# Retention attention and an ELU feed-forward on one Trainium2 core: order of state matmuls and bank copies, the pipeline of the first batch, and how block-diagonal states are written

## The chip, the cores and the metric

The kernel runs on one core of a Trainium2 chip. The metric is device time in microseconds for one execution; lower is better. The engines in the profile are PE (TensorE, matmuls; PEld is its weight load), DVE (VectorE), ACT (ScalarE), POOL (GpSimd) and SP (SyncE, which here only issues DMAs).

## The reference

```python
def _attn_ref(q, k, v):                     # 8 batches, 8 heads, 576 positions, 64 wide
    scores = scale * np.matmul(q, k.transpose(0, 1, 3, 2))
    gamma = 1.0 - 2.0 ** (-5.0 - np.arange(H, dtype=np.float32))
    Dmat = np.where(rel >= 0, gamma[:, None, None] ** rel[None, :, :], 0.0)
    ret = scores * Dmat[None, :, :, :]
    return np.matmul(ret, v).astype(np.float32)

def _moe_ref(x, w_in, w_out):               # 4608 tokens, 512 -> 2048 -> 512
    h = x @ w_in
    g = np.where(h > 0.0, h, alpha * (np.exp(np.minimum(h, 0.0)) - 1.0))
    return (g @ w_out).astype(np.float32)
```

The heads of the attention output are put side by side, so that x is 4608 x 512. The attention has no softmax: scores are multiplied by a decay that depends on the distance alone and vanishes above the diagonal.

## The kernel before

**Attention in units.** Because the decay gamma^(i-j) splits into gamma^i times gamma^-j, queries and keys are scaled once and the causal product becomes linear. A batch is cut into five units: four of 256 positions by four heads (`T` is 0 or 1 for the half of the sequence, `w` is 0 or 1 for the half of the heads) and a tail of 64 positions with all eight heads. Forty units in all; units 0 to 3 are the first batch without its tail, unit 4 (`FT`) is that tail, units 5 to 8 the second batch. Within a unit of 256 positions there are two chunks of 128 (`c` is 0 or 1). Each position's output is the masked product within its chunk (`scores`, `masks`, `values`) plus the queries times the sum of k·v over all earlier chunks (`inter`). `state` computes k·v of the unit's two chunks, `prefix` adds them to the running total: `mid` is the sum up to the middle of the unit, `end` up to its end, both on DVE. They are then written in bf16 as block-diagonal matrices of two heads (`s_mid`, `s_end`), whose other blocks were set to zero once at the beginning, so that `inter` handles two heads in one matmul.

**What a unit goes through.** `load` issues three DMAs for q, k and v on SP. `cast` scales q and k by the decay tables into bf16 (`qkn`, two instructions each, one for every `e`) and converts v (`vn`); without `split` all on POOL, with it q on DVE and v on the engine that `split` names, issued later by `later[u]`. `turn_pe` transposes q and k by TensorE through a bank of `ps_h` and copies them out (`qkT`; q on DVE, k on ACT); from unit 9 on `turn` does it by a transposing DMA instead.

**Banks.** `x0` and `x1` hold the unit's output (columns 0 to 255) and the states (columns 256 to 383) in the same bank, one buffer each (`ps_x`); `sc` has one buffer, `ps_h` three, `ps_m` one. Dependences are kept by bank: a TensorE write into a bank waits for the reads of it that came before. `put_x` (line 319) copies both output banks to `xt`, the transposed x of the feed-forward, normally on ACT.

**Order.** All matmuls are pinned in program order through `mm`. `soft` pins the other engines' instructions too as long as `early[0]` is true, that is up to `finish(FT + 2)` at line 537; from then on a planner places the instructions of DVE, ACT and POOL by its own estimate of when they are ready. Each engine runs its queue strictly in that order. All DMAs on SP are pinned.

**The stages.** (1) Lines 472 to 499: the first batch, one unit a round; `warm` issues matmuls on zeros between them. `last_of_start` finishes unit 3 in two halves of heads. (2) Lines 500 to 519: 16 pieces of w_in and 16 of w_out come through eight staging buffers (`wst`) and are converted on POOL, while `ffn1` and `ffn2` of the first 512 tokens run. (3) Lines 520 to 537: the rest of that group's `ffn2`, with units 4, 5 and 6 between. (4) From line 538: `ffn1` of the second group in two parts, then groups of 512 tokens, in which `step` (line 561) puts a unit's `stretch` between the slots of feed-forward matmuls. In `stretch(u)` the matmuls of unit u and of unit u-1's output are issued together: inter(u-1), scores(u), values(u-1), then the copies `put_x(u-1)`, then state(u) and prefix(u).

Of the kernel before, what the change touches and what calls it, by code (L numbers as in the profile page):

```python
# [17 lines left out]
def kernel(  # L18
# [15 lines left out]
    P = 128  # L34
# [33 lines left out]
    def soft(ins):  # L68
        return pin(ins) if early[0] else ins
# [57 lines left out]
                            channel_multiplier=-1)  # L127


    s_mid, s_end = [], []  # L130
    for i in range(2):
        for lst, n in ((s_mid, 1), (s_end, 2)):
            row = []
            for j in range(n):
                s = const.tile([P, 2, P], BF16, name=f"sbd{i}{j}{n}")
                nc.gpsimd.memset(s, 0.0)
                row.append(s)
            lst.append(row)

    w_in_sb = const.tile([P, KJ, DF], BF16, name="w_in_sb")  # L140
    w_out_sb = const.tile([P, NFT, DM], BF16, name="w_out_sb")
# [13 lines left out]
        soft(engines[eng](w_out_sb[:, f, :], t))  # L155


    rawt, natt, trt, ptt, score_ps, later, total = {}, {}, {}, {}, {}, {}, {}
# [6 lines left out]
    def load(u):  # L165
        if u >= NS:
            return
        b, T, w, tail = unit(u)
        if tail:
            rqk = raw.tile([P, H, D], FP32, name="rqt", tag="rqt", bufs=2)  # L170
            rv = raw.tile([ST, H, D], FP32, name="rvt", tag="rvt", bufs=2)
            for dst, src in ((rqk[:ST], q), (rqk[ST:], k), (rv, v)):
                pin(nc.sync.dma_start(dst, src[b, :, FT * P :, :].rearrange("h p d -> p h d")))
        else:
            rqk = raw.tile([P, 2, 4, 2, D], FP32, name="rqk", tag="rqk")
            rv = raw.tile([P, 4, 2, D], FP32, name="rv", tag="rv")
            for dst, src in ((rqk[:, 0], q), (rqk[:, 1], k), (rv, v)):
# [6 lines left out]
    def cast(u, split=None):  # L184
        if u >= NS:
            return
        b, T, w, tail = unit(u)
        rqk, rv = rawt.pop(u)
        if tail:
            qkn = nat.tile([P, H, D], BF16, name="qkt", tag="qkt", bufs=2)  # L190
            vn = nat.tile([ST, H, D], BF16, name="vt", tag="vt", bufs=2)
            g = gq[:, FT].unsqueeze(2).to_broadcast([P, H, D])
            for hs in (slice(0, H // 2), slice(H // 2, H)):
                soft(nc.gpsimd.tensor_tensor(qkn[:, hs], rqk[:, hs], g[:, hs], ALU.mult))
            soft(nc.gpsimd.tensor_copy(vn, rv))
        else:
            qkn = nat.tile([P, 2, 2, 4, D], BF16, name="qkn", tag="qkn")
            vn = nat.tile([P, 4, 2, D], BF16, name="vn", tag="vn", bufs=5)
            for i, tab in enumerate((gq, gk)):
                eng = nc.vector if split and i == 0 else nc.gpsimd  # L200
                x = rqk[:, i].rearrange("p h e d -> p e h d")
                g = tab[:, 2 * T : 2 * T + 2, 4 * w : 4 * w + 4].unsqueeze(3).to_broadcast([P, 2, 4, D])
                for e in range(2):
                    soft(eng.tensor_tensor(qkn[:, i, e], x[:, e], g[:, e], ALU.mult))  # L204
            later[u] = lambda: soft(engines[split or "p"](vn, rv))  # L205
            if not split:
                later.pop(u)()
        natt[u] = qkn, vn

    def turn_tile(u):  # L210
        n = 4 if unit(u)[3] else 8
        trt[u] = tpool.tile([P, n, P], BF16, name="qkT", tag=f"qkT{n}")
        return n
# [6 lines left out]
            turn_tile(u)  # L220
            pin(nc.sync.dma_start_transpose(trt[u], flat(u)))

    def turn_pe(u, parts=(0, 1)):
        n = turn_tile(u) if 0 in parts else 8
        for i in parts:
            if i * 4 < n:
                p = ps_h.tile([P, 4, P], BF16, name="ptr", tag="ph")
                for j in range(4):
                    lo = (i * 4 + j) * P
                    pin(nc.tensor.transpose(p[:, j], flat(u)[:, lo : lo + P], ident))  # L230
                soft(engines["vs"[i]](trt[u][:, i * 4 : i * 4 + 4], p))  # L231

    def queries(u, rows, hl, c):

# [52 lines left out]
    def inter(u, hls=(0, 1), to=None):  # L287
        b, T, w, tail = unit(u)
        if tail:
            for hp in range(HP):  # L290
                o = xps[0][:, hp * ST : (hp + 1) * ST]
                acc_x(0, 2, o, s_end[hp // 2][1][:, hp % 2], trt[u][:, hp, :ST])
            return
        for c in range(2):
            if T + c == 0:
                continue
            s = s_mid[w][0] if c else s_end[w][0]
# [39 lines left out]
    def drop(u):  # L337
        natt.pop(u)
        ptt.pop(u)
        trt.pop(u)  # L340
# [9 lines left out]
                        o = 2 * P + hl * D  # L350
                        acc_x(c, i, xps[c][i * D : (i + 1) * D, o : o + D], qkn[cs, 1, e, 2 * hl + i], vn[cs, 2 * hl + i, e])

    def prefix(u):
        b, T, w, tail = unit(u)
        st = [x[:, 2 * P : 3 * P].rearrange("p (h d) -> p h d", h=2) for x in xps]
        mid = rpool.tile([P, 2, D], FP32, name="mid", tag="mid")
        end = rpool.tile([P, 2, D], FP32, name="end", tag="end")
        if T == 0:
            soft(nc.vector.tensor_copy(mid, st[0]))
        else:  # L360
            soft(nc.vector.tensor_tensor(mid, st[0], total[w], ALU.add))  # L361
        soft(nc.vector.tensor_tensor(end, st[1], mid, ALU.add))
        total[w] = end
        for dst, src in ((s_mid[w][0], mid), (s_end[w][T], end)):
            for i in range(2):
                r = slice(i * D, (i + 1) * D)
                soft(nc.gpsimd.tensor_copy(dst[r, :, r], src[r]))  # L367

    def last_of_start(u):

        sc = score_ps.pop(u)
        pt = ppool.tile([P, 2, 2, 2 * P], BF16, name="pt", tag="pt")
        ptt[u] = pt
        second = [ps_h.tile([P, 512], FP32, name="o2", tag="ph") for _ in range(2)]
        for hl in range(2):
            soft(nc.vector.tensor_tensor(
                pt[:, :, hl], sc.rearrange("p i (h n) -> p i h n", h=2)[:, :, hl],
                mask.rearrange("p k e r -> p (k e r)").unsqueeze(1).to_broadcast([P, 2, 2 * P]), ALU.mult,
            ))
# [90 lines left out]


    for u in range(FT):
        load(u)
    cast(0, split="s")
    turn_pe(0)
    scores(0)
    later.pop(0)()
    new_x()
    state(0)
    prefix(0)  # L480
    for u in range(1, FT):
        cast(u, split="p" if u == FT - 1 else "s")
        masks(u - 1)
        warm(2)
        turn_pe(u, (0,))
        new_x()
        inter(u - 1)
        values(u - 1)
        put_x(u - 1)
        drop(u - 1)  # L490
        turn_pe(u, (1,))
        later.pop(u)()
        warm(1)
        scores(u)
        state(u)
        prefix(u)
    warm(2)
    new_x()
    last_of_start(FT - 1)
    for i in range(6):  # L500
        w_in_piece(i, "p")
# [123 lines left out]
```

## Time and profile before

| | us |
|---|---|
| median of three runs (370.94 to 371.69) | 371.31 |
| profiled execution, whole | 371.33 |
| its span on the core | 369.6 |

The profile counts from the start of the span. Its page gives busy times by engine, the waits tell what released an engine that stood, and a timeline row has the start, the time, the engine, the line of the source, what is written from what, the number of instructions, and in brackets how long the engine had been idle and what ended it. A row with several instructions is their merged time. Line 72 is the helper through which every matmul goes, so matmuls are told apart by the names of their tiles: `x<-vn,qkn` is state, `x<-pt,vn` values, `x<-qkT,sbd` inter, `sc<-qkT` scores, `ph` ffn1, `pm` ffn2.

### The profile page before, as it was taken

What the parts mean: (1) busy time and instruction counts of PE and PEld (TensorE: products, weight loads), DVE (VectorE), ACT (ScalarE), POOL (GpSimd) and SP (SyncE); (2) the same over time, 40 slices, a digit from 0 to 9 for tenths busy, and PEclk for the clock granted to TensorE, in tenths of its full rate; (3) what the DMA queues carried; (4) which work ended last, traced back from release to release, by engine and by line L of the source; (5) the groups of instructions that cost most, each with busy time, mean ns of one, the idle gap of its engine ahead of it and who ended that gap; (6) DMA issues with size and microseconds to landing.
All of it is one profiled execution on the core that took longest, in us unless ns stands there. A gap on an engine that the chain in (4) does not pass through costs nothing.

```text
span 369.6 us, 7943 instructions
## 1 busy us (share of the span) xinstructions
PE 318.6 (86%) x3044; PEld 161.4 (44%) x3087; DVE 203.2 (55%) x380; ACT 176.1 (48%) x360; POOL 180.7 (49%) x385
## 2 busy tenths in 40 slices
PE   3779996287877899999999999999999999999995
PEld 1443443144555444444444444444444444444442
DVE  3546725167574777556556666655655565454500
ACT  3226632156443655655555555555555555655511
POOL 6558955984699687056553665366511110010000
PEclk9978999679899999999999999999999999999999
DMA  7908999984799987906559656932220000010012
GB/s 222 330 22 253 394 267 299 268 185 113 185 202 222 276 136 209 231 29 101 145 148 185 155 170 145 235 89 77 67 65 28 30 31 29 28 58 29 28 61 83
DMA packets 100294, 53.87 MB, mean 146 GB/s; under 512 B 44448, under 2 KB 93600, under 8 KB 100256
## 3 DMA queue, kind: packets, MB, share of 16 engines
q1 hardware_dynamic: 97696, 44.97, 50.4%
q0 software_dynamic: 2560, 8.39, 6.1%
q8 instruction: 24, 0.39, 0.5%
q14 instruction: 14, 0.11, 0.1%
HBM read 36.70 MB, written 9.44 MB: 125 GB/s over the span
## 4 chain that ended last, share of the span: by engine, by line
PE 69%; POOL 11%; ACT 9%; DVE 5%; issue 4%; DMA 2%; DVEq 0%; POOLq 0%; ACTq 0%
PE ph L72 30%; PE pm L72 30%; PE x L72 6%; POOL qkn L204 4%; ACT xt L334 4%; PE sc L72 3%; DMA wst<-in_moe_w_in_dram 2%; ACT ot L453 1%; POOL w_in_sb L150 1%; ACT ph L434 1%; DVE pt L281 1%; POOL vn L205 1%; ACT qkT L231 1%; DVE g L443 1%; DVE em L436 1%
## 5 line engine op out<-in xcount | busy, mean ns | idle before, releaser
L72 PE MATMUL ph<-xt,w_in_sb 128*128 128x512 bf16 (+2 forms) x612 | 149.4, 365 | 3.7 <-DVE g L443 0.9
L72 PE MATMUL pm<-w_out_sb,g 128*128 128x512 bf16 x564 | 142.7, 379 | 2.9 <-ACT ot L453 1.5
L432 ACT ACTIVATE e<-ph 128x512 f32<-128x512 f32 (+2 forms) x152 | 87.3, 574 | 116.8 <-PE ph L72 103.1
L72 PEld LDWEIGHTS <-w_in_sb 128*128 128x128 bf16 x640 | 60.1, 99 | 66.1 <-issue 4.5
L72 PEld LDWEIGHTS <-g 128*128 128x128 bf16 x576 | 55.7, 98 | 70.4 <-issue 7.1
L441 DVE SCALAR_TENSOR_TENSOR g<-e,ph 128x512 bf16<-128x512 f32 (+2 forms) x80 | 50.3, 633 | 59.3 <-ACT ph L434 58.6
L456 POOL DMA_DIRECT2D out_dram<-ot x32 | 18.1, 566 | 98.1 <-ACT ot L453 71.6
L436 DVE TENSOR_SCALAR em<-e 128x512 bf16<-128x512 f32 (+2 forms) x76 | 36.0, 474 | 51.4 <-ACT e L432 51.4
L443 DVE SCALAR_TENSOR_TENSOR g<-ph,em 128x512 bf16<-128x512 f32 (+2 forms) x80 | 50.6, 637 | 3.2
L434 ACT ACTIVATE ph<-ph 128x512 f32<-128x512 f32 (+2 forms) x76 | 43.3, 570 | 0.0
L334 ACT CAST xt<-x 128x256 bf16<-128x256 f32 (+1 forms) x72 | 24.1, 414 | 38.2 <-PE x L72 38.1
L204 POOL TENSOR_TENSOR qkn<-rqk,gk 128x256 bf16<-128x256 f32 x64 | 40.2, 635 | 3.5
L281 DVE TENSOR_TENSOR pt<-sc,mask 128x1024 bf16<-128x1024 f32 x31 | 37.8, 1218 | 7.0 <-PE sc L72 7.0
L204 POOL TENSOR_TENSOR qkn<-rqk,gq 128x256 bf16<-128x256 f32 x52 | 31.1, 618 | 13.4 <-PE x L72 13.3
L453 ACT COPY ot<-pm 128x512 f32<-128x512 f32 x36 | 21.1, 589 | 21.8 <-PE pm L72 21.8
L205 POOL CAST vn<-rv 128x512 bf16<-128x512 f32 x29 | 18.2, 629 | 23.9 <-PE x L72 19.7
L72 PE MATMUL x<-vn,qkn 64*64 64x64 bf16 x512 | 15.0, 205 | 16.2 <-ACT xt L334 10.9
L72 PEld LDWEIGHTS <-qkn 64*64 64x64 bf16 x512 | 12.4, 114 | 21.5 <-issue 20.2
L72 PE MATMUL sc<-qkT 64*64 64x128 bf16 (+1 forms) x576 | 16.8, 229 | 4.7 <-ACT qkT L231 4.2
L230 PE MATMUL ptr<-ident,qkn 128*128 128x128 bf16 x64 | 8.9, 252 | 10.3 <-DVE qkn L204 5.6
L367 POOL CAST sbd_149<-mid 64x128 bf16<-64x128 f32 x32 | 10.2, 317 | 13.8 <-DVE mid L361 7.2
L72 PE MATMUL x<-pt,vn 64*64 64x128 bf16 x504 | 14.0, 228 | 1.7 <-DVE pt L281 1.7
(77 smaller groups left out, 181.1 us busy)
## 6 DMA issues: line engine op xcount, KB each, us to landing
rqk<-in_q_dram SPq DMA_DIRECT2D x32, 256.0 KB, 4.5
rqk<-in_k_dram SPq DMA_DIRECT2D x32, 256.0 KB, 4.9
rv<-in_v_dram SPq DMA_DIRECT2D x32, 256.0 KB, 5.1
out_dram<-ot POOLq DMA_DIRECT2D x32, 256.0 KB, 2.5
wst<-in_moe_w_in_dram SPq DMA_DIRECT2D x16, 256.0 KB, 5.1
wst<-in_moe_w_out_dram SPq DMA_DIRECT2D x16, 256.0 KB, 4.8
rqt<-in_q_dram SPq DMA_DIRECT2D x8, 128.0 KB, 3.9
rqt<-in_k_dram SPq DMA_DIRECT2D x8, 128.0 KB, 3.4
```

Source lines behind the costliest of these rows:

```text
L72: pin(nc.tensor.matmul(*a, **kw))
L204: soft(eng.tensor_tensor(qkn[:, i, e], x[:, e], g[:, e], ALU.mult))
L205: later[u] = lambda: soft(engines[split or "p"](vn, rv))
L281: soft(nc.vector.tensor_tensor(pt.rearrange("p i h n -> p (i h) n"), sc.rearrange("p i (h n) -> p (i h) n", h=2), mask.rearrange("p k e r ...
L334: soft(engines[eng[c]](dst, src[:, :, :, a // 2 : (a + n) // 2]))
L432: soft(nc.scalar.activation(e[:, :m], ph[:, :m], AF.Exp))
L434: soft(nc.scalar.activation(ph[:, :m], ph[:, :m], AF.Relu))
L436: soft(nc.vector.tensor_scalar_add(em[:, :m], e[:, :m], -1.0))
L441: soft(nc.vector.scalar_tensor_tensor(dst, e[:, c], -1.0, ph[:, c], ALU.add, ALU.min))
L443: soft(nc.vector.scalar_tensor_tensor(dst, ph[:, c], 0.0, em[:, c], ALU.max, ALU.min))
L453: soft(nc.scalar.copy(ot, pm))
L456: soft(store.dma_start(out[i0 : i0 + P, :], ot))
```

## The change

Four things change. In `stretch`, state(u) is issued ahead of put_x(u-1). `prefix` writes each block-diagonal state by one multiply with a 0/1 table that is broadcast over the blocks, instead of two copies of the diagonal blocks; the six memsets of whole matrices go. The first batch runs in a loop in which unit u+1 is transposed and unit u+2 cast during unit u, with v casts on ACT and both transposed halves copied by ACT (for unit 0 as before); the last unit's prefix runs on DVE. In the second batch's start, casts of units 4, 5 and 6 are issued earlier and spread over POOL, DVE and ACT, the tail's load stands ahead of w_out, and the third tile's `ffn2` is cut in two around unit 4.

```diff
-                s = const.tile([P, 2, P], BF16, name=f"sbd{i}{j}{n}")
-                nc.gpsimd.memset(s, 0.0)
+    s_mid = [const.tile([P, 2, P], BF16, name=f"s_mid{w}") for w in range(2)]
+    s_end = [[const.tile([P, 2, P], BF16, name=f"s_end{w}{t}") for t in range(2)] for w in range(2)]
+    diag = const.tile([P, 2], FP32, name="diag")
+    nc.gpsimd.memset(diag, 0.0)
+    nc.gpsimd.memset(diag[:D, :1], 1.0)
+    nc.gpsimd.memset(diag[D:, 1:], 1.0)
...
+            parts = [(rqk[:, 0], q), (rqk[:, 1], k), (rv, v)]
+            for dst, src in parts[2:] + parts[:2] if last else parts:
...
+    def cast_q(u, eng, i=0):
+        b, T, w, tail = unit(u)
+        x = rawt[u][0][:, i].rearrange("p h e d -> p e h d")
+        g = (gq, gk)[i][:, 2 * T : 2 * T + 2, 4 * w : 4 * w + 4].unsqueeze(3).to_broadcast([P, 2, 4, D])
+        for e in range(2):
+            soft(eng.tensor_tensor(natt[u][0][:, i, e], x[:, e], g[:, e], ALU.mult))
+
+    def cast(u, q="p", v="p"):
...
+            cast_q(u, nc.vector if q == "v" else nc.gpsimd)
+            cast_q(u, nc.gpsimd, 1)
+            if v:
+                cast_v(u, v)
...
+    def cast_v(u, eng):
+        soft(engines[eng](natt[u][1], rawt[u][1]))
...
-    def turn_pe(u, parts=(0, 1)):
+    def turn_pe(u, eng="vs"):
...
-    def prefix(u):
+    def prefix(u, eng=nc.gpsimd):
...
-        for dst, src in ((s_mid[w][0], mid), (s_end[w][T], end)):
-            for i in range(2):
-                r = slice(i * D, (i + 1) * D)
-                soft(nc.gpsimd.tensor_copy(dst[r, :, r], src[r]))
+        for dst, src in ((s_mid[w], mid), (s_end[w][T], end)):
+            soft(eng.tensor_tensor(
+                dst.rearrange("p h (j d) -> p h j d", j=2), src.unsqueeze(2).to_broadcast([P, 2, 2, D]),
+                diag.unsqueeze(1).unsqueeze(3).to_broadcast([P, 2, 2, D]), ALU.mult,
+            ))
...
     def last_of_start(u):
-        second = [ps_h.tile([P, 512], FP32, name="o2", tag="ph") for _ in range(2)]
+        both = [[ps_h.tile([P, 512], FP32, name="o2", tag="ph") for _ in range(2)], None]
         for hl in range(2):
...
-            to = second if hl else None
-            inter(u, (hl,), to)
-            values(u, (hl,), to)
-            put_x(u, (hl,), to, ("ss", "sv")[hl])
+            if hl == 0:
+                prefix(u, nc.vector)
+            else:
+                new_x()
+            values(u, (hl,), both[hl])
+            inter(u, (hl,), both[hl])
+            put_x(u, (hl,), both[hl], ("ss", "sv")[hl])
...
     def stretch(u):
...
         if late:
             values(u - 1)
+        if u < NS and not unit(u)[3]:
+            state(u)
+        if late:
             put_x(u - 1)
             drop(u - 1)
         if u < NS and not unit(u)[3]:
-            state(u)
             prefix(u)
...
+        load(u, last=(u == FT - 1))
+    cast(0, "v", None)
     turn_pe(0)
+    cast(1, "v", None)
+    for u in range(FT):
+        scores(u)
+        cast_v(u, "s")
+        if u + 1 < FT:
+            turn_pe(u + 1, "ss")
+        new_x()
+        if u:
+            inter(u - 1)
+            values(u - 1)
+        state(u)
+        warm(2)
+        if u + 1 < FT:
+            masks(u)
+            prefix(u)
+        if u:
+            put_x(u - 1)
+            drop(u - 1)
+        if u + 2 < FT:
+            cast(u + 2, "v", None)
     last_of_start(FT - 1)
...
     for ft in range(8):
+        if ft == 0:
+            load(FT)
...
-    for u in range(FT, FT + 6):
+    for u in range(FT + 1, FT + 6):
         load(u)
+    cast(FT)
+    cast(FT + 1, "v", "s")
     for ft in range(8, 16):
...
-    cast(FT)
-    for part in Q:
+    for part in Q[:2]:
         ffn2(0, 2, part)
     turn_pe(FT)
     stretch(FT)
-    cast(FT + 1, split="p")
-    later.pop(FT + 1)()
+    for part in Q[2:]:
+        ffn2(0, 2, part)
+    cast(FT + 2, "v", "s")
     ffn2(0, 3, Q[0])
     ffn2(0, 3, Q[1])
     turn_pe(FT + 1)
     stretch(FT + 1)
-    cast(FT + 2, split="p")
-    later.pop(FT + 2)()
```

More of the change, by code (lines that the diff above doesn't have):

```diff
@@ L155, in w_out_piece @@
         soft(engines[eng](w_out_sb[:, f, :], t))
-    rawt, natt, trt, ptt, score_ps, later, total = {}, {}, {}, {}, {}, {}, {}
+    rawt, natt, trt, ptt, score_ps, total = {}, {}, {}, {}, {}, {}
     xps, begun = [None, None], set()
@@ L163, in unit, with load @@
         return b, r // 2, r % 2, r == FT
-    def load(u):
+    def load(u, last=False):
         if u >= NS:
@@ L176, in load @@
             rv = raw.tile([P, 4, 2, D], FP32, name="rv", tag="rv")
-            for dst, src in ((rqk[:, 0], q), (rqk[:, 1], k), (rv, v)):
+            parts = [(rqk[:, 0], q), (rqk[:, 1], k), (rv, v)]
+            for dst, src in parts[2:] + parts[:2] if last else parts:
                 pin(nc.sync.dma_start(
@@ L187, in cast @@
         b, T, w, tail = unit(u)
-        rqk, rv = rawt.pop(u)
+        rqk, rv = rawt[u]
         if tail:
@@ L198, in cast @@
             vn = nat.tile([P, 4, 2, D], BF16, name="vn", tag="vn", bufs=5)
[L199 to L207, printed above, removed]
+            natt[u] = qkn, vn
+            cast_q(u, nc.vector if q == "v" else nc.gpsimd)
+            cast_q(u, nc.gpsimd, 1)
+            if v:
+                cast_v(u, v)
         natt[u] = qkn, vn
+    def cast_v(u, eng):
+        soft(engines[eng](natt[u][1], rawt[u][1]))
     def turn_tile(u):
@@ L221, in turn @@
             pin(nc.sync.dma_start_transpose(trt[u], flat(u)))
-    def turn_pe(u, parts=(0, 1)):
-        n = turn_tile(u) if 0 in parts else 8
-        for i in parts:
+    def turn_pe(u, eng="vs"):
+        n = turn_tile(u)
+        for i in range(2):
             if i * 4 < n:
@@ L296, in inter @@
                 continue
-            s = s_mid[w][0] if c else s_end[w][0]
+            s = s_mid[w] if c else s_end[w][0]
             x = (to or xps)[c]
@@ L472 @@
     for u in range(FT):
-        load(u)
-    cast(0, split="s")
+        load(u, last=(u == FT - 1))
+    cast(0, "v", None)
     turn_pe(0)
[L476 to L483, printed above, removed]
-        warm(2)
[L485 to L498, printed above, removed]
+    cast(1, "v", None)
[9 more added lines that the diff above has]
+        state(u)
+        warm(2)
+        if u + 1 < FT:
[6 more added lines that the diff above has]
+            cast(u + 2, "v", None)
     last_of_start(FT - 1)
```

10 lines of the change are left out of this document (1 added, 9 removed).

## The prediction

> **What bounds the kernel now.** I read the page first, then windows by stage, then TensorE's waits, then the timeline at each place where TensorE stands.
>
> ```profile
> span 369.6 us, 7943 instructions
> PE 318.6 (86%) x3044; PEld 161.4 (44%) x3087; DVE 203.2 (55%) x380; ACT 176.1 (48%) x360; POOL 180.7 (49%) x385
> 0.00:24.00 24.00, 13.51 (x191) 7.28 (x193) 10.77 (x38) 7.56 (x17) 13.90 (x45) 1.00 0.75 219
> 68.00:74.00 6.00, 0.77 (x18) 0.52 (x18) 1.15 (x3) 0.30 (x1) 5.88 (x13) 0.53 0.91 271
> 104.00:120.00 16.00, 11.32 (x222) 7.73 (x215) 9.13 (x20) 6.59 (x17) 15.09 (x35) 1.00 1.16 217
> 120.00:320.00 200.00, 186.60 (x1831) 92.91 (x1856) 122.93 (x208) 107.78 (x216) 90.53 (x195) 1.00 0.50 121
> ```
>
> The window columns are length, then busy time of PE, PEld, DVE, ACT and POOL, then granted clock, DMA share, GB/s. Three regimes show. From 120 to 320 TensorE is the bound (186.6 of 200 us). From 104 to 120 POOL is (15.09 of 16). Before that, in the first 24 us and again at 68 to 74, no engine but POOL in the latter is near full: those are chains of latencies.
>
> In the long stage TensorE's idle time has two names:
>
> ```profile
> PE x L72 <- ACT xt L334: 8.1, 15, 0.6
> PE x L72 <- ACT xt L323: 2.5, 5, 0.5
> 127.99 0.39 PE L72 MATMUL x<-pt,vn 64*64 64x128 bf16 x16
> 128.42 0.75 ACT L334 CAST xt<-x 128x256 bf16<-128x256 f32 x2
> 128.92 0.62 PE L72 MATMUL x<-vn,qkn 64*64 64x64 bf16 x16 [0.54 <-ACT xt L334]
> 157.36 0.32 PE L72 MATMUL x<-vn,qkn 64*64 64x64 bf16 x16 [0.51 <-ACT xt L323]
> ```
>
> The first two rows are waits of 120 to 320 (total us, times, longest). The state matmuls (`x<-vn,qkn`) write the banks that put_x is copying out, so they wait. Behind the copy of two banks, the 16 matmuls also take 0.62 instead of 0.32 us: the first two use bank 0, the rest stand until bank 1 is copied as well. So a normal unit costs 0.54 + 0.30, a unit behind a tail 0.51.
>
> **The change part by part.** The sum is made against the profiled execution, 371.33 us (span 369.6 plus 1.73 around it), within 0.02 of the median.
>
> *Step 1, state ahead of the copies (120 to 320).* One order of TensorE's queue changes; nothing is added. 15 × (0.54 + 0.30) + 5 × 0.51 = 15.1 us of standing go. What is late next: put_x now waits for 0.3 us of state, and `xt` is needed a group later, so nothing. ACT and DVE do the same work in 185 instead of 200 us, 58% and 66%. I leave 0.6 for stalls on `ph` banks where the elementwise work is dense: **14.5** (11 if ACT's copies hold up the exponentials after half of the units by about 0.4 us, 16 if the other 3 us of idle shrink too).
>
> *Step 2, first batch (0 to 27.6).*
>
> ```profile
> 5.07 0.30 POOL L136 MEMSET sbd_159<- 128x256 bf16 x1
> 5.35 1.18 POOL L204 TENSOR_TENSOR qkn<-rqk,gk 128x256 bf16<-128x256 f32 x2
> 6.58 0.40 PE L230 MATMUL ptr<-ident,qkn 128*128 128x128 bf16 x2 [0.18 <-POOL qkn L204]
> 7.66 0.64 PE L72 MATMUL sc<-qkT 64*64 64x128 bf16 x16 [0.68 <-ACT qkT L231]
> 8.17 0.43 PE L72 MATMUL x<-vn,qkn 64*64 64x64 bf16 x16
> 8.64 0.29 DVE L359 COPY mid<-x 128x128 f32<-128x128 f32 x1 [3.21 <-PE x L72]
> 10.33 0.42 PE L72 MATMUL x<-qkT,sbd_149 128*128 128x128 bf16 x2
> 11.27 0.64 PE L72 MATMUL x<-pt,vn 64*64 64x128 bf16 x16 [0.52 <-DVE pt L281]
> 13.20 0.64 PE L72 MATMUL sc<-qkT 64*64 64x128 bf16 x16 [0.32 <-ACT qkT L231]
> 24.23 0.64 PE L72 MATMUL sc<-qkT 64*64 64x128 bf16 x16 [0.59 <-ACT qkT L231]
> 26.42 0.68 DVE L376 TENSOR_TENSOR pt<-sc,mask 128x512 bf16<-128x512 f32 x1
> 27.60 5.38 PE L72 MATMUL ph<-xt,w_in_sb 128*128 128x512 bf16 x16
> ```
>
> Today three rounds take 24.23 − 7.66 = 16.6 us, 5.5 each, and scores(0) waits for a key cast that stands behind six memsets (six times about 0.25 start to start); these go, against three tiny ones: scores(0) at about 6.7. State(0) now stands behind the cast (1.2) and the transposes (0.4) of unit 1's keys: it ends at 8.2 if they have landed by 5.6, and I take 9.2, for a landing near 6.6 that no row shows. In the new order masks, query casts and scores lie beside the round; what closes it is state(u) → mid 0.35 → two multiplies on POOL → keys of u+2 on POOL, queued behind them, 1.2 → last transposes 0.4 → inter 0.3, values 0.6, state 0.4 (starts a little overlapped). The multiply is not in the trace: bounds are the cast pair it replaces (0.74 here) and two 128x256 POOL multiplies (1.18). I take 1.18, the same shape and operands: 4.4 us a round.
>
> POOL may also be slowed, since DVE casts the queries just then:
>
> ```profile
> 57.41 2.04 POOL L204 TENSOR_TENSOR qkn<-rqk,gk 128x256 bf16<-128x256 f32 x2
> 57.66 0.74 DVE L204 TENSOR_TENSOR qkn<-rqk,gq 128x256 bf16<-128x256 f32 x2
> 9.07 0.74 POOL L367 CAST sbd_149<-mid 64x128 bf16<-64x128 f32 x2 [2.54 <-DVE mid L359]
> 9.24 0.85 DVE L204 TENSOR_TENSOR qkn<-rqk,gq 128x256 bf16<-128x256 f32 x2
> ```
>
> Beside DVE's cast POOL's pair took 2.04 instead of 1.18; the single-input casts at 9.07 lost only about 0.1. So the round is 4.4 to 5.3 us; I take 4.85, the middle. The Trainium skill (SBUF — State Buffer, section "Who interferes with whom") says that a DVE instruction with two SBUF inputs and a GpSimd one that reads SBUF contend, the later one blocked for the whole instruction. The first pair of rows agrees with it, the second hardly; by the rule alone the round would be 5.3 and the gain 0.9 us smaller.
>
> State(2) ends at 9.2 + 2 × 4.85 = 18.9. Then two idle-filling matmuls and scores(3) 1.5, inter, values, state 1.3, mid and end 0.7, two multiplies on DVE 0.85 (as the query pair at 9.24), half a mask 0.7, last values 0.3: 5.4, so FFN starts at 24.3 instead of 27.6 (23.4 and 25.2 by the two rounds, half a us more either way for the keys): **3.3** (1.9 to 4.7).
>
> *Step 3, weights (27.6 to 52.3).*
>
> ```profile
> 26.93 7.13 POOL L150 CAST w_in_sb<-wst 128x512 bf16<-128x512 f32 x12
> 29.00:30.00 1.00, 1.00 (x3) 0.28 (x3) 0.00 (x0) 0.08 (x1) 1.00 (x3) 0.50 0.92 248
> 38.70 0.59 PE L72 MATMUL pm<-w_out_sb,g 128*128 128x512 bf16 x2 [0.39 <-POOL w_out_sb L155]
> ```
>
> The last unit's multiplies move to DVE, so POOL may begin the weight casts after prefix(2), about 19.7 instead of 26.93, and SyncE, which waits for freed staging buffers, fetches the rest 7 us earlier. The unit-4 load, three small DMAs, now stands ahead of w_out; that cover is 3 us. TensorE still pays the half clock of its first microseconds and the same elementwise work; only the pacing at 29 us and the 0.39 go: **0.8** (0 to 1.5).
>
> *Step 4, second batch's start (52.27 to 74.76).*
>
> ```profile
> 52.27 3.61 PE L72 MATMUL pm<-w_out_sb,g 128*128 128x512 bf16 x16 [0.46 <-ACT ot L453]
> 65.34 0.29 PE L230 MATMUL ptr<-ident,qkn 128*128 128x128 bf16 x2 [1.46 <-POOL qkn L204]
> 66.87 0.42 PE L72 MATMUL sc<-qkT 64*64 64x128 bf16 x16 [0.56 <-ACT qkT L231]
> 72.05 1.17 POOL L194 TENSOR_TENSOR qkt<-rqt,gq 128x256 bf16<-128x256 f32 x2
> 73.18 0.63 POOL L367 CAST sbd_155<-mid 64x128 bf16<-64x128 f32 x2
> 73.87 0.39 PE L72 MATMUL x<-qkT,sbd_155 128*128 128x128 bf16 x2 [5.10 <-POOL sbd_155 L367]
> 74.76 0.72 PE L72 MATMUL ph<-xt,w_in_sb 128*128 128x320 bf16 x2
> ```
>
> TensorE waits for casts (1.46 and others) and 5.10 us for prefix(6), which the planner put behind casts that are not yet needed. With casts of units 4 to 6 moved up and spread to DVE and ACT, their cover is the 3.5 us of second matmuls ahead of them. New path: 32 matmuls 7.2, three turns of 1.1 (transposes 0.4, then the wait of 0.56 for the copy, and a latency) 3.3, scores 1.15, values and state 1.3, a wait for `ot` that the new order exposes 0.5 (as the 0.46), mask → mid → multiply behind the last scores 1.5 beyond what values and state cover, last inter and values 0.6: 15.6; with 1.1 for latencies and POOL's queue 16.7 against 22.5: **5.8** (0.7 if the 5.1 return, 6.9).
>
> *Step 5, 75 to 98 and 98 to 120.* One normal unit's wait (0.84) and some half clock after the 5.1 us hole (0.53 granted in the row above) go: **1.4** (0.5 to 3). [...] From 98 to 120 about 3.2 us of such waits stand before POOL, which has no room, so POOL's order decides: **1.0** (−1 if the multiplies come later than the four small casts, 3.5).
>
> Sum 14.5 + 3.3 + 0.8 + 5.8 + 1.4 + 1.0 = 26.8; 371.3 − 26.8 = **344.5 us**.
>
> **The rivals.**
> - *POOL's order repeats.* Unpinned casts again stand before prefix(6). For it: the 5.10 row, and the planner is the same. Against: POOL is free some 7 us longer beforehand. One such wait: 349.6. Chance 0.15.
> - *POOL stands for the whole of DVE's cast.* 2.04 − 1.18 = 0.86 more in every round, 5.3: FFN at 25.2, 345.4. Chance 0.10, the two pairs of rows speaking against each other. The Trainium skill's rule of step 2 is this case.
> - *A second bound.* In the long stage ACT and DVE hold up TensorE as soon as it no longer stands; half of 14.5 comes back: 351.8. Against: 54% and 61% busy. Chance 0.09.
> - *The order doesn't do it.* State still waits for a copy, or scores do instead: step 1 gives nothing, 359. Chance 0.03.
> - *Slower.* From unit 7 on nothing pins the multiplies; if each block-diagonal state came behind prefetch casts as at 73.18, each next inter would stand 5.1 us. 26.8 / 5.1 = 5.3: from six of the 24 later units on the kernel is slower; at six 375. Against, TensorE's waits from 104 to 120, the only ones of this kind behind 76:
>
> ```profile
> PE x L72 <- POOL sbd_155 L367: 1.1, 2, 0.9
> PE x L72 <- POOL sbd_149 L367: 1.1, 1, 1.1
> ```
>
> Chance 0.03.
>
> **How the numbers follow.** The forecast has 0.60 and its own terms' ends make 339 to 350, since not all fall on one side. The range reaches over POOL's order and part of the second bound: 338.5 to 352.5. This kernel's measurements tell about 0.2% (0.7 us) from no change. Faster 0.96; within 0.01; slower 0.03 is the last rival.
>
> **What would show it.** Right: no row "PE x L72 <- ACT xt" in the new waits from 100 on, state beginning within 0.1 us of values; first 512-wide `ph` near 24; w_in casts on POOL from about 20; first 320-wide `ph` near 65. Wrong: PE waiting for POOL's `s_mid` again, POOL multiplies near 1 us each, or `ph` matmuls waiting for DVE `g` in the long stage.

## The result, and the profile after

The changed kernel takes **357.9 us** (median of four runs, 355.8 to 359.5) against 371.5 for the kernel before, run beside it: ratio 0.9627, interval 0.9573 to 0.9681. The forecast was 344.5 with a range of 338.5 to 352.5, so the direction was right and the size was not: about half of the forecast gain came. Medians and ranges here and below are of all runs of a kernel; a run over 1.5% above the fastest of its kernel counts as slow (the 350.6 of `e1_pool_order`, the 362.7 and 362.8 of `e7_order_to_120`), and ratios and intervals leave those out. The profiled execution is the fastest of the four, 355.82 us, 15.5 under the profiled 371.33 of before.

Where the gain stayed out is read first from the start of each stage. The starts are those of the first matmul of the stage in TensorE's timeline:

| step of the prediction | stage before, us | forecast gain | stage after, us | gain |
|---|---|---|---|---|
| 2: first batch | 0 to 27.60 | 3.3 | 0 to 25.33 | 2.3 |
| 3: weights | 27.60 to 52.27 | 0.8 | 25.33 to 50.30 | −0.3 |
| 4: second batch's start | 52.27 to 74.76 | 5.8 | 50.30 to 71.61 | 1.2 |
| 5: 320-wide stage | 74.76 to 95.88 | 1.4 | 71.61 to 92.66 | 0.1 |
| 5: 192-wide stage | 95.88 to 120.03 | 1.0 | 92.66 to 117.88 | −1.1 |
| 1: long stage | 120.03 to 369.6 | 14.5 | 117.88 to 354.1 | 13.3 |

The windows of the kernel after, by these stages (length; busy time of PE, PEld, DVE, ACT and POOL; granted clock; DMA share; GB/s):

```profile
25.30:36.70 11.40, 11.11 (x37) 4.25 (x37) 6.71 (x12) 6.84 (x13) 5.80 (x10) 0.75 1.04 249
50.30:71.60 21.30, 11.30 (x170) 6.45 (x171) 6.72 (x12) 4.33 (x9) 19.34 (x33) 0.85 1.13 266
117.90:354.00 236.10, 225.96 (x2031) 110.35 (x2059) 154.41 (x235) 128.16 (x252) 93.93 (x159) 0.99 0.47 113
```

and the long stage of the kernel before in the same view:

```profile
120.00:369.60 249.60, 231.12 (x2031) 112.70 (x2059) 139.20 (x235) 127.84 (x252) 93.23 (x200) 1.00 0.43 106
```

Three things stand out. From 50 to 72 TensorE is busy for 11.3 us of 21.3, and POOL for 19.3. At the start of the first multiplications the clock is 0.75 on average. And in the long stage VectorE does the same 235 instructions in 154 us in place of 139.

TensorE's waits in the kernel after, 120 us to the end (total us, times, longest):

```profile
PE x L72 <- POOL s_mid_149 L369: 2.1, 1, 2.1
PE ph L72 <- DVE g L453: 1.5, 2, 1.4
PE pm L72 <- ACT ot L463: 1.0, 2, 0.8
```

The 20 waits for `xt` (15 and 5 from 120 to 320 before) are gone: that is where the 13.3 us come from. But over the whole run a new name has come:

```profile
PE x L72 <- POOL s_mid_150 L369: 10.5, 4, 5.9
PE x L72 <- POOL s_mid_149 L369: 6.8, 4, 2.2
```

Together 17.3 us, where the kernel before had 7.3 of the kind (6.2 and 1.1 for `sbd`). The timeline of the kernel after shows the two longest of them:

```profile
63.87 0.28 PE L72 MATMUL x<-qkT,s_mid_149 128*128 128x128 bf16 x2 [2.17 <-POOL s_mid_149 L369]
...
65.69 0.28 DVE L363 COPY mid<-x 128x128 f32<-128x128 f32 x1
66.08 1.19 POOL L187 TENSOR_TENSOR qkn<-rqk,gk 128x256 bf16<-128x256 f32 x2
67.20 0.61 POOL L212 CAST vn<-rv 128x512 bf16<-128x512 f32 x1
67.77 1.17 POOL L187 TENSOR_TENSOR qkn<-rqk,gq 128x256 bf16<-128x256 f32 x2
68.92 1.17 POOL L187 TENSOR_TENSOR qkn<-rqk,gk 128x256 bf16<-128x256 f32 x2
70.06 0.60 POOL L369 TENSOR_TENSOR s_mid_150<-mid,diag 128x256 bf16<-128x256 f32 x1
70.71 0.40 PE L72 MATMUL x<-qkT,s_mid_150 128*128 128x128 bf16 x2 [5.87 <-POOL s_mid_150 L369]
```

`mid` is there at 65.97. The multiply that TensorE waits for takes 0.60 us, as forecast, but it stands behind seven casts of later units and begins at 70.06. The wait of 5.10 that the prediction set out to remove came back as 5.87, and one of 2.17 stands ahead of it.

### The profile page after: what moved, and what is told of

The parts are those of the page before. It is cut to its first block, busy times and chain, and to the rows that moved or that the text cites. A ratio compares the mean times of both kernels' runs of the same rounds, so it can differ in the third digit from the quotient of the medians.

```text
span 354.1 us, 7848 instructions
## 1 busy us (share of the span) xinstructions
PE 310.5 (88%) x3040; PEld 157.0 (44%) x3084; DVE 219.8 (62%) x379; ACT 180.5 (51%) x366; POOL 177.2 (50%) x313
## 4 chain that ended last, share of the span: by engine, by line
PE 65%; POOL 12%; DMA 9%; issue 5%; DVE 4%; ACT 2%; SPq 2%; POOLq 0%; ACTq 0%; DVEq 0%
PE pm L72 29%; PE ph L72 28%; POOL qkn L187 6%; PE x L72 5%; DMA rqk<-in_k_dram 3%; DVE em L446 3%; PE sc L72 3%; DMA rvt<-in_v_dram 2%; DMA rv<-in_v_dram 2%; DMA wst<-in_moe_w_out_dram 1%; POOL w_in_sb L147 1%; POOL vn L212 1%; SPq L176 1%; POOL s_mid_149 L369 1%; POOL s_mid_150 L369 1%
## 5 line engine op out<-in xcount | busy, mean ns | idle before, releaser
L72 PEld LDWEIGHTS <-w_in_sb 128*128 128x128 bf16 x640 | 60.9, 100 | 68.4 <-issue 11.1
L446 DVE TENSOR_SCALAR em<-e 128x512 bf16<-128x512 f32 (+2 forms) x76 | 53.0, 697 | 36.3 <-ACT e L442 35.8
L338 ACT CAST xt<-x 128x256 bf16<-128x256 f32 (+1 forms) x71 | 24.2, 417 | 39.9 <-PE x L72 38.3
L187 POOL TENSOR_TENSOR qkn<-rqk,gq 128x256 bf16<-128x256 f32 x52 | 31.1, 617 | 14.9 <-PE x L72 13.6
L212 POOL CAST vn<-rv 128x512 bf16<-128x512 f32 x26 | 16.3, 626 | 22.8 <-PE x L72 22.8
L72 PEld LDWEIGHTS <-qkT 64*64 64x64 bf16 x576 | 10.5, 113 | 9.9 <-ACT qkT L235 3.1
L369 POOL TENSOR_TENSOR s_mid_149<-mid,diag 128x256 bf16<-128x256 f32 x16 | 10.0, 622 | 8.4 <-DVE mid L365 6.3
L369 POOL TENSOR_TENSOR s_mid_150<-mid,diag 128x256 bf16<-128x256 f32 x15 | 9.1, 607 | 9.7 <-DVE mid L363 6.5
```

Source lines behind the costliest of these rows:

```text
L72: pin(nc.tensor.matmul(*a, **kw))
L187: soft(eng.tensor_tensor(natt[u][0][:, i, e], x[:, e], g[:, e], ALU.mult))
L212: soft(engines[eng](natt[u][1], rawt[u][1]))
L338: soft(engines[eng[c]](dst, src[:, :, :, a // 2 : (a + n) // 2]))
L369: soft(eng.tensor_tensor(dst.rearrange("p h (j d) -> p h j d", j=2), src.unsqueeze(2).to_broadcast([P, 2, 2, D]), diag.unsqueeze(1).unsque ...
L446: soft(nc.vector.tensor_scalar_add(em[:, :m], e[:, :m], -1.0))
```

## The experiments

All runs were timed beside the kernel before, whose median was 372.0 to 372.2 in them.

**POOL's order.** If the misplaced multiplies are the cause, it is enough to hold POOL to the order in which the program writes its work: each `soft` of the casts and of the multiplies becomes `pin`.

```diff
-            soft(eng.tensor_tensor(natt[u][0][:, i, e], x[:, e], g[:, e], ALU.mult))
+            pin(eng.tensor_tensor(natt[u][0][:, i, e], x[:, e], g[:, e], ALU.mult))
...
-            soft(eng.tensor_tensor(
+            pin(eng.tensor_tensor(
                 dst.rearrange("p h (j d) -> p h j d", j=2), src.unsqueeze(2).to_broadcast([P, 2, 2, D]),
```

> The changed kernel (357.9 us) with every cast and every block-diagonal multiply pinned, so that POOL's queue is program order and no cast for a later unit stands ahead of a multiply. Theory 'POOL's order': TensorE's waits for the multiplies in the changed kernel (2.2 and 5.9 us at 64 and 71, 7.2 us from 90 to 120, 2.1 at 137) go for the most part: 346 to 350 us. Rival 'POOL is full': the same work in another order gives at most 2 us, 356 to 358, and the waits come back as waits for casts.

Measured: 345.7 us (343.9 to 350.6), ratio 0.9269, interval 0.9213 to 0.9324. The theory holds, and the time is a little under its 346 to 350: by the two ratios (0.9627 and 0.9269) some 13 us come back, and no engine has one instruction more or less. TensorE's waits for the multiplies on POOL fall from 17.3 to 2.9 us. The same place in this run's timeline:

```profile
66.77 0.28 DVE L363 COPY mid<-x 128x128 f32<-128x128 f32 x1
67.14 0.60 POOL L369 TENSOR_TENSOR s_mid<-mid,diag 128x256 bf16<-128x256 f32 x1 [1.65 <-DVE mid L363]
67.80 0.29 PE L72 MATMUL x<-qkT,s_mid 128*128 128x128 bf16 x2 [1.88 <-POOL s_mid L369]
```

POOL now waits for `mid` and not the other way round; 1.88 us is what is left of the wait when nothing stands ahead of the multiply. The 320-wide stage begins at 68.37 (71.61 in the kernel after), and the long stage shrinks too:

```profile
114.00:345.00 231.00, 224.19 (x2031) 109.64 (x2059) 143.28 (x235) 128.25 (x252) 104.26 (x173) 1.00 0.55 125
```

**The parts by themselves.** The kernel after with the old order of copies and states in `stretch`, the rest of the change kept:

```diff
-        if u < NS and not unit(u)[3]:
-            state(u)
         if late:
             put_x(u - 1)
             drop(u - 1)
         if u < NS and not unit(u)[3]:
+            state(u)
             prefix(u)
```

> The changed kernel with only the order in stretch put back (put_x ahead of state). If step 6 was right (about 14 us in the long stage), 371 to 373 us, that is nothing left of the change. If the long stage was shortened by something else, under 363.

Measured: 368.6 (367.0 to 369.2), ratio 0.9890. It lies somewhat under the 371 to 373 expected (the "step 6" of the expectation is step 1 of the prediction). So the order of states is worth 10.7 us in the changed kernel, and all the rest of the change 3.4 without it.

The kernel before with that order alone:

```diff
         if late:
             values(u - 1)
+        if u < NS and not unit(u)[3]:
+            state(u)
+        if late:
             put_x(u - 1)
             drop(u - 1)
         if u < NS and not unit(u)[3]:
-            state(u)
             prefix(u)
```

> The kernel before (371.5 us) with only state ahead of put_x. Theory: 13 to 16 us less, 355 to 358, so that the other three parts together give about nothing. Rival: the parts share the gain, and this alone gives under 9 us, over 362.

Measured: 356.5 (354.3 to 357.2), ratio 0.9565, interval 0.9515 to 0.9614. One moved call of `state` does what the whole change does, whose interval (0.9573 to 0.9681) overlaps it. The rest of the change, with 9.9 us of forecast in steps 2 to 4 alone, brings nothing on top of it that can be measured here. In this run too POOL's order takes a part: TensorE's waits for the block copies are 15.2 us, where the kernel before had 7.3:

```profile
PE x L72 <- POOL sbd L367: 15.2, 7, 5.7
```

**The masked multiply.** The kernel after with two block copies for each state again, the zeros set by VectorE:

```diff
-            soft(eng.tensor_tensor(
-                dst.rearrange("p h (j d) -> p h j d", j=2), src.unsqueeze(2).to_broadcast([P, 2, 2, D]),
-                diag.unsqueeze(1).unsqueeze(3).to_broadcast([P, 2, 2, D]), ALU.mult,
-            ))
+            for i in range(2):
+                r = slice(i * D, (i + 1) * D)
+                soft(eng.tensor_copy(dst[r, :, r], src[r]))
```

> The changed kernel with the block-diagonal states written by two copies of the diagonal blocks each, as before, the zeros set on DVE; all else as changed. Theory 'POOL's order': the order stays, so 356 to 360 us. Rival 'the multiplies block DVE': the conversions em that took 6.28 and 2.7 us instead of 0.43 behind POOL's unbroken queue become short again and 2 to 5 us go, 353 to 356.

Measured: 354.8 (352.9 to 357.1), ratio 0.9532, interval 0.9475 to 0.9589. That is in the range of the rival, and its sign is there too: the conversion `em` of VectorE, which had taken up to 6.28 us, takes 1.77 at the most. One group of the list of this run (the same group of the other kernels is shown further down):

```profile
L443 DVE TENSOR_SCALAR em<-e 128x512 bf16<-128x512 f32 (+2 forms) x76 | 41.4, 544 | 40.3 <-ACT e L439 40.0
```

TensorE's waits for the `g` of line 453 (line 450 here) fall from 2.2 to 0.4 us. The gain itself is shown weakly, since the intervals touch and the two profiled executions differ by 0.5 us only (355.8 and 355.3): the long stage is 1.9 us shorter (234.3), the 192-wide stage 1.5 longer (26.7). So the same edit was made where the planner has no say, on `e1_pool_order`:

```diff
+            for i in range(2):
+                r = slice(i * D, (i + 1) * D)
+                pin(eng.tensor_copy(dst[r, :, r], src[r]))
```

> The kernel after with POOL held to the order of the program and with two block copies for each state in place of the masked multiply. If the multiplies cost time of their own (they take the port from VectorE): 342 to 344.5. If e4's 3 us were only another order of POOL: 345 to 347, as e1_pool_order.

Measured: 346.3 (345.1 to 349.1), ratio 0.9301, interval 0.9271 to 0.9331, against 0.9213 to 0.9324 with the multiplies. So with the order held the multiply costs nothing that shows. With the planner's order it goes with longer conversions on VectorE; how much of e4's 3 us is that and how much another order of POOL stays open.

**The other two parts, with the order held.** The kernel before with the state ahead of the copies and POOL pinned; old first batch, old start of the second batch, old block copies (the edit of e3, and this, with the casts of the tails in the same way):

```diff
-                    soft(eng.tensor_tensor(qkn[:, i, e], x[:, e], g[:, e], ALU.mult))
-            later[u] = lambda: soft(engines[split or "p"](vn, rv))
+                    pin(eng.tensor_tensor(qkn[:, i, e], x[:, e], g[:, e], ALU.mult))
+            later[u] = lambda: pin(engines[split or "p"](vn, rv))
...
-                soft(nc.gpsimd.tensor_copy(dst[r, :, r], src[r]))
+                pin(nc.gpsimd.tensor_copy(dst[r, :, r], src[r]))
```

> The kernel before with two edits: the state matmuls ahead of the copies (as in e3_state_first_only) and the casts and block copies of POOL held to the order of the program. The old first batch, the old block copies and the old start of the second batch stay. Theory (POOL's order is what cost the forecast gain, and the first batch's pipeline and the second batch's start are worth little by themselves): 345 to 349, within 3 of e1_pool_order. Rival (with the order right, the first batch and the start of the second batch bring the 3.3 and 5.8 that I gave them): 352 to 356, 6 or more above e1_pool_order.

Measured: 347.9 (347.5 to 348.4), ratio 0.9355, interval 0.9333 to 0.9378. Two edits to the old kernel come within 2 to 3 us of `e1_pool_order` (2.1 by the medians, 3 by the ratios, whose intervals don't touch). Its stages: multiplications from 27.81, third tile from 52.59, 320-wide stage from 70.17. So its second batch's start takes 17.6 us, where the kernel before took 22.5 and e1 15.3. Of the 7.2 us between the kernel before and e1, 2.3 are the new start and 4.9 the two edits: 0.5 the order of states (this stage takes 21.95 us in e3) and 4.4 POOL's order.

**Half an order.** Pinned only up to unit 9 (the expectation counts one too many), so that the long stage keeps the planner's order:

```diff
+    def hold(u, ins):
+        return pin(ins) if u <= FT + 5 else soft(ins)
...
-    soft(eng.tensor_tensor(natt[u][0][:, i, e], x[:, e], g[:, e], ALU.mult))
+    hold(u, eng.tensor_tensor(natt[u][0][:, i, e], x[:, e], g[:, e], ALU.mult))
```

> The kernel after with POOL held to the order of the program for units 5 to 10 alone (casts of units up to 10, states of units up to 10), so the long stage keeps the planner's order. Theory (the misplaced multiplies of 50 to 120 us cost some 4 us, and the stretches where POOL runs without a gap in the long stage the other 5): the 512-wide stage near 120 begins at 113.5 to 115, the time is 351 to 354. Rival (the long stage's loss comes with what is misplaced before it): 345 to 348.

Measured: 360.6 (356.5 to 362.8), ratio 0.9613: neither case, and by the ratio the time of the kernel after (0.9627). In the profiled execution (362.8) the first half went well, the 320-wide stage began at 67.97 (68.37 in e1). But the 512-wide stage began at 122.65 and not at 113.5 to 115: the free casts of the units from 10 on were drawn ahead of a pinned multiply. That order is fixed in the program; the length of the wait is this execution's:

```profile
85.10 0.28 DVE L368 TENSOR_TENSOR mid<-x,end 128x128 f32<-128x128 f32 x1
86.95 1.17 POOL L190 TENSOR_TENSOR qkn<-rqk,gq 128x256 bf16<-128x256 f32 x2
...
94.32 0.60 POOL L190 TENSOR_TENSOR qkn<-rqk,gk 128x256 bf16<-128x256 f32 x1
94.89 0.61 POOL L372 TENSOR_TENSOR s_mid<-mid,diag 128x256 bf16<-128x256 f32 x1
95.55 0.40 PE L72 MATMUL x<-qkT,s_mid 128*128 128x128 bf16 x2 [9.34 <-POOL s_mid L372]
```

Pinning an instruction keeps it behind the pinned ones ahead of it; it keeps nothing free from passing it. That is also why the multiplies at 63 and 70 us of the kernel after, which are pinned, came late: the casts of unit 7 and beyond are not. What this experiment can't tell is the long stage's own share, since this wait lies ahead of it.

**The half clock.** Four 512-wide matmuls of no use in each of the two stands of TensorE at the end of the first batch:

```diff
+        d = ps_h.tile([P, TG], FP32, name="warm", tag="ph")
...
+            if hl:
+                for _ in range(4):
+                    mm(d, ident, zero, start=True, stop=True)
             values(u, (hl,), both[hl])
+            if not hl:
+                for _ in range(4):
+                    mm(d, ident, zero, start=True, stop=True)
             inter(u, (hl,), both[hl])
```

> The kernel after with eight 512-wide matmuls of no use set into the two stands of TensorE at the end of the first batch (four ahead of the state matmuls of the first half, four ahead of the values of the second). If the half clock at the start of the first multiplications comes from TensorE standing there: the granted clock is 1.00 from 25 us on, the first eight first-half multiplications take 9.4 to 9.8 us again (11.2 in the kernel after), and the time is 354 to 357. If the clock falls for another reason: the stage takes 11 to 11.4 us and the time is 357 to 359.

Measured: 360.0 (358.0 to 362.0), ratio 0.9680, outside both ranges. The cause is confirmed and the gain isn't there. Windows of the kernel after:

```profile
22.00:24.00 2.00, 0.73 (x11) 0.34 (x10) 1.81 (x4) 0.96 (x4) 2.00 (x4) 1.00 0.57 167
26.00:28.00 2.00, 2.00 (x6) 0.72 (x5) 0.09 (x1) 0.60 (x1) 1.39 (x3) 0.50 0.88 207
```

and with the warming matmuls:

```profile
26.00:28.00 2.00, 2.00 (x11) 0.86 (x10) 0.81 (x2) 1.12 (x3) 2.00 (x4) 1.00 0.91 215
```

Eleven matmuls in 2 us in place of six, at clock 1.00 in place of 0.50, and the first eight first-half multiplications take 9.2 us in place of 11.2. In all six profiled executions with the new first batch and without these matmuls (the kernel after, e1, e2, e4, e6, e7) the clock fell there, in the three with them (e8, e9, e10) it didn't. With the old first batch it fell in the kernel before, but not in e3 and e5, so a half clock there is no fixed cost. But TensorE then meets the second half's weights before they are there:

```profile
37.65 4.66 POOL L152 CAST w_out_sb<-wst 128x512 bf16<-128x512 f32 x7 [2.48 <-DMA wst<-in_moe_w_out_dram]
38.32 0.95 PE L72 MATMUL pm<-w_out_sb,g 128*128 128x512 bf16 x2 [3.40 <-POOL w_out_sb L152]
```

TensorE waits for POOL, and POOL itself stood 2.48 us for the transfer. Behind this wait the clock fell again (0.60 from 38 to 40 us, 0.54 from 40 to 42). In the kernel after the wait was 0.2: TensorE came there 1.6 us later (36.55 for 34.92), by the half clock, and the first cast of w_out began 1.6 us earlier (36.07).

**A version that takes both.** `e1_pool_order` with the warming matmuls, ten staging buffers for the weights in place of eight, and the load of unit 4 behind the weights' loads:

```diff
-    wst = ctx.enter_context(tc.tile_pool(name="wst", bufs=8))
+    wst = ctx.enter_context(tc.tile_pool(name="wst", bufs=10))
...
-        if ft == 0:
-            load(FT)
...
-    for u in range(FT + 1, FT + 6):
+    for u in range(FT, FT + 6):
         load(u)
```

> e1_pool_order with the eight warming matmuls of e8_warm_end, ten buffers for the weights on their way in place of eight, and the load of the second batch's first unit behind the weights' loads in place of ahead of the second half of them. Theory (once TensorE begins the multiplications at full clock, they wait for the weights, whose transfers run without a gap from 23 us on; two pieces more loaded early and 0.4 MB less ahead of w_out take some 2.5 to 3 us off that wait): the first w_out multiplication begins at 35 to 36 without a wait of over 1 us, the third tile begins at 49.5 to 50.5 (53.0 in e1), the time is 342 to 344. Rival (the weights' arrival isn't the bound, POOL's casts are, or what is saved is lost at the second batch's late load): the third tile at 52 or later, 345 to 347.

Measured: **341.1 us** (340.7 to 341.5), ratio 0.9158, interval 0.9137 to 0.9179: faster than both kernels and, by 1 us, than the theory. The second half's weights are there in time, from POOL's and TensorE's timelines:

```profile
32.81 8.63 POOL L152 CAST w_out_sb<-wst 128x512 bf16<-128x512 f32 x13
35.52 0.59 PE L72 MATMUL pm<-w_out_sb,g 128*128 128x512 bf16 x2
```

and the third tile begins at 49.82 (53.04 in e1).

Last, in `step` the transposing DMA ahead of the next loads:

```diff
         stretch(u)
+        turn(u + 2)
         load(u + 5)
         cast(u + 3)
-        turn(u + 2)
```

> e9_warm_and_weights, and in the long stage the transposing DMA of the unit after next is issued ahead of the next loads in place of behind them. Theory (the transposes stand on SP's queue behind loads that wait for a buffer, which is what TensorE's 5.5 us of waits for qkT between 90 and 115 in e1 are): those waits fall under 2 us, the time is 2.5 to 4 under e9_warm_and_weights. Rival (the transposes wait for their casts on POOL, which is the bound there): the waits stay, the time is within 1 of e9_warm_and_weights.

Measured: 340.6 (337.4 to 341.6), ratio 0.9139, interval 0.9106 to 0.9172: the same as without it, so the rival has the time. TensorE's waits from 90 to 115:

```profile
PE x L72 <- POOL s_mid L369: 3.0, 3, 1.5
PE sc L72 <- DMA qkT<-qkn: 2.2, 2, 1.3
```

The waits for `qkT` had already shrunk in e9, from e1's 5.5 to 2.9 over the same stage (84 to 109 us there), beside 2.5 for `s_mid`, so the run says little about SP's queue. What is left there is most likely POOL's, which is busy for 23.4 of these 25.1 us in e9, as the prediction read it for 104 to 120.

## Why the prediction was wrong, step by step

With POOL's order held, each step can be measured as the prediction meant it. Gains against the profiled 371.33, by the same stage starts, in the one profiled execution of each kernel:

| step | forecast | after | e1, order held | e9, also weights |
|---|---|---|---|---|
| 2: first batch | 3.3 | 2.3 | 2.4 | 1.3 |
| 3: weights | 0.8 | −0.3 | −3.2 | 1.1 |
| 4: second batch's start | 5.8 | 1.2 | 7.2 | 7.2 |
| 5: 320-wide | 1.4 | 0.1 | 1.9 | 2.1 |
| 5: 192-wide | 1.0 | −1.1 | −2.3 | −0.9 |
| 1: long stage | 14.5 | 13.3 | 18.6 | 19.0 |
| sum | 26.8 | 15.5 | 24.6 | 29.8 |

**Step 4 is where it failed**, with 4.6 of the 11.3 us that are missing. The prediction saw the 5.10 row, read it rightly as the planner's order, and then let the new code remove it. Its rival, POOL's order repeating, got a chance of 0.15 on the ground that POOL would be free some 7 us longer beforehand. That ground was no cover: POOL uses free time for whichever casts the planner ranks first, and loads had come early enough to feed it (19.34 of 21.3 us busy). The rival's price was low too, one wait where two came, 2.17 + 5.87 = 8.0. Without them the stage would be 21.3 − 8.0 = 13.3 us, and e1's is 15.3 − 1.9 = 13.4, so these waits are the whole difference. The path was right: e1's 15.3 us, with the 1.88 that is left of the wait, stand against 16.7 worked out with 1.5 for it. That POOL would be free for the multiply was wrong. Over all stages holding the order brings 9.1 of the missing 11.3 us back (24.6 for 15.5), though step 3 loses 2.9 more there.

**Step 5** fails by the same order: the 320-wide stage gained 0.1 for 1.4, the 192-wide one lost 1.1 for a gain of 1.0. The "−1 if the multiplies come later than the four small casts" is what came. Waits for multiplies take 1.6 us in the first stage (one) and 5.6 in the second (four). Nor did the half clock go that the prediction put down to the hole of 5.10 us. It reached 3.8 us into the 320-wide stage before (to 78.6) and 3.7 after (to 75.3). It had not come from that hole: before, the clock fell at 68.3, ahead of the hole, which began at 68.8. With the order held, the 192-wide stage still loses: there TensorE stood 5.5 us for `qkT` in e1, and e9 still loses 0.9. POOL has little room in it (busy for 24.2 of 26.4 us in e1), as the prediction said, so what other stages gain is partly given back here.

**Step 1** was right in mechanism and near in size, 13.3 for 14.5. The order alone gives 15.5 (e3's long stage takes 234.1 us in place of 249.6). It was cut by what POOL's order did next to VectorE. One group of each run's list, in the order before, after, e1:

```profile
L436 DVE TENSOR_SCALAR em<-e 128x512 bf16<-128x512 f32 (+2 forms) x76 | 36.0, 474 | 51.4 <-ACT e L432 51.4
```

```profile
L446 DVE TENSOR_SCALAR em<-e 128x512 bf16<-128x512 f32 (+2 forms) x76 | 53.0, 697 | 36.3 <-ACT e L442 35.8
```

```profile
L446 DVE TENSOR_SCALAR em<-e 128x512 bf16<-128x512 f32 (+2 forms) x76 | 41.4, 545 | 34.2 <-ACT e L442 33.9
```

Five of the 76 instructions of the kernel after make most of the 17 us; the longest is below, and it holds TensorE up for 1.36 us. With the 2.1 for `s_mid` above, and half clock behind these stands (0.50 from 138 to 140 us), that is most of the 5.2 us by which e1's long stage is shorter. With block copies and the planner's order (e4) four of the five places take 1.59 to 1.77 us, and at the fifth no `em` takes over 1.2. So both signs that the prediction named under "wrong" came, PE waiting for `s_mid` and for `g`; but it is not the second bound of the rivals, it is a few long instructions.

**Step 2** came to 2.3 for 3.3, inside its range. Timeline of the kernel after:

```profile
9.71 0.43 PE L72 MATMUL x<-vn,qkn 64*64 64x64 bf16 x16
14.26 0.43 PE L72 MATMUL x<-vn,qkn 64*64 64x64 bf16 x16
18.80 0.43 PE L72 MATMUL x<-vn,qkn 64*64 64x64 bf16 x16
22.69 0.69 DVE L369 TENSOR_TENSOR s_mid_150<-mid,diag 128x256 bf16<-128x256 f32 x1
23.30 0.82 DVE L369 TENSOR_TENSOR s_end_154<-end,diag 128x256 bf16<-128x256 f32 x1
25.33 1.06 PE L72 MATMUL ph<-xt,w_in_sb 128*128 128x512 bf16 x2
```

State(0) ends at 10.14, 0.9 later than the 9.2 taken. The rounds are 4.55 us, within the 4.4 to 5.3 and better than the 4.85 taken, which gives 0.6 back over two. VectorE's two multiplies take 1.43 from the start of the first to the end of the second in place of 0.85: 0.6. Together 0.9 of a miss of 1.0. State(0) was late because unit 1's keys, taken to land near 6.6, came at 8.14 (POOL's key cast begins there, after a wait for the DMA). The rival in which POOL stands for the whole of DVE's cast (5.3 a round) is refuted: in a round VectorE's query pair lies beside POOL's multiplies and takes 1.41 in place of 0.76, and POOL's key pair behind them takes 1.36 in place of 1.18, not the 2.04 of the rival. The prediction's row at 57.41 didn't show the later of the two blocked either: POOL's pair began first, 0.25 us ahead of VectorE's, and was the one lengthened.

**Step 3** came to −0.3 for 0.8, and two of its premises failed. The first is that TensorE pays the same half clock as before. In the kernel before the clock was back at full from 30.8, 3.2 us into the stage; in the kernel after from 30.9, 5.6 us into it. The second is that the weights are covered. POOL began the weight casts 6.1 us earlier (20.82, near the forecast), but the first cast of w_out came only 2.0 earlier, at 36.07 for 38.04, after a stand of 2.79 for its transfer. This bound is the stronger one: in e1 the half clock reached only 2.5 us into the stage and in e8 there was none, yet the stage took 27.8 us in both, nearly 3 more than in the kernel after. There w_out was cast from 37.12 and 37.65 on, TensorE waited 2.30 and 3.40 us for it, and the clock fell again behind the wait. Why w_out came later in them than in the kernel after stays open. e9 moved it and has the 1.1.

The chance of 0.60 on the forecast rested on the planner choosing well in four stages. The range left out what the 5.10 row already showed it to do. (A slip without consequence: the last rival counts 24 later units with a multiply, there are 26.)

## What to carry to other kernels

A wait that a profile names by its releaser is gone only when that releaser's queue is settled too: a producer that a planner orders freely, fed by early loads, will stand behind work that nobody needs yet, and here fixing the order of one engine (13 us) was worth as much as the whole change (13.6). Half an order brought nothing (e7): a pin orders only the pinned, and what is free still goes ahead of them. And look at what comes next on a chain that is shortened: at the end of the first batch the clock, and behind it a transfer, took the gain back until both were moved (e8, e9).

## What the hardware showed that was not expected

VectorE's `em`, one input and a constant, 0.43 us when alone, can last as long as POOL's queue runs without a gap. Timeline of the kernel after, with the rows of POOL on both sides and TensorE's wait:

```profile
134.91 1.18 POOL L187 TENSOR_TENSOR qkn<-rqk,gq 128x256 bf16<-128x256 f32 x2
135.22 6.28 DVE L446 TENSOR_SCALAR em<-e 128x512 bf16<-128x512 f32 x1 [0.36 <-ACT e L442]
...
140.04 1.17 POOL L187 TENSOR_TENSOR qkn<-rqk,gk 128x256 bf16<-128x256 f32 x2
...
143.28 1.02 PE L72 MATMUL ph<-xt,w_in_sb 128*128 128x512 bf16 x4 [1.36 <-DVE g L453]
```

It starts while POOL works and ends at 141.50, just after POOL's first pause, at 141.21, behind eleven POOL instructions without a gap. Four others took 2.72 to 2.83 us in the same way. The Trainium skill (SBUF — State Buffer, section "Who interferes with whom") says that such an operation can take the port pair that VectorE and GpSimd share, and that the one which comes second is blocked for the whole instruction of the other. The trace agrees on the block, but its length here is that of a queue, not of one instruction. In e1 POOL ran as long without a gap around 138 us and the same operation took 0.90 and 0.54 there, with POOL's pair 0.18 longer: which of the two gives way is not settled by these runs.

The granted clock fell to half though TensorE was not idle. In the kernel after it fell at 24.1, and in the 3.4 us before that TensorE had been busy for 1.9 (0.50 and 0.23 us in the last two); eight matmuls of no use kept it at 1.00. How long it stays down isn't fixed, but it comes in steps: from 24.1 to 30.9 there and from 24.0 to 30.8 in the kernel before, 6.8 us; from 24.3 to 27.7 in e1 and for as long in e2, e6 and e7, 3.4 us, half of it.
